# Q of five batches transposed by the DMA engines instead of by TensorE, with a new hand-written order, in a linear-attention and gated-FFN kernel

## Chip, cores and metric

The kernel runs on one core of one Trainium2 chip. The metric is the device time of one execution in microseconds. A profiled execution also has a span, from its first to its last instruction, which leaves out what lies around it.

## What is computed

There are 8 batches, 8 heads, 576 positions and a head dimension of 64. Cut to what matters:

```python
kv   = einsum('bhsd,bhse->bhde', k, v)          # per head 64 x 64
out  = einsum('bhsd,bhde->bhse', q, kv)
out  = out / sqrt(mean(out*out, -1) + 1e-6) * g_norm
x    = out.transpose(0, 2, 1, 3).reshape(B, S, 512)
h    = maximum(x @ w_in, 0)                     # 512 -> 1024
conv = sum over k of conv_w[k] * h[s + k - 1]   # 3 taps along the positions
y    = (h * sigmoid(conv)) @ w_out              # 1024 -> 512, float32
```

## The kernel before

All matmuls are in bfloat16 with float32 sums in PSUM. Features lie on the 128 partitions and positions along the free axis, so that two heads (a "pair" t of 0 to 3) fill the partitions. The work on a batch b is cut into small operations, each a function with a short name. A string ORDER (L64 to L109) lists them in the order in which they are recorded (the loop at L656), and a dependency from each instruction to the one before it on its engine (L661 to L669) keeps every engine's queue in just that order. The order comes from a planner; no engine passes one instruction by to run a later one. So a wait in any instruction holds all that stands behind it on its engine.

The operations, by the names in ORDER:

- `Lq.b`, `Lk.b.u`, `Lv.b.u` (L149 to L155) load q, k and v of a batch from DRAM. GpSimd's queue (POOL) issues them, and they cast float32 to bfloat16 on the way: one load reads 1,152 KB and writes 576 KB to 96 partitions, with six neighbouring positions in each partition's row. There are two buffers each for q, k and v, so the load of batch b waits until batch b-2 has been read.
- `qt.b.u` (L328 to L337) transposes q of four heads on TensorE, 24 matmuls against an identity into a PSUM tile of the pool `ps_a`. `qc.b.u` (L340) is VectorE's copy of it to SBUF, into a buffer named qT (four of them).
- `kv.b.t0.n` (L283) makes k-transposed times v, 12 matmuls for each pair, in PSUM. `kvc.b.t0.n.i` (L297) is ScalarE's copy of the two 64 x 64 diagonal blocks of each pair into a block-diagonal 128 x 128 matrix `kvbd`.
- `ot.b.t` (L351) makes the product of a pair: one 128 x 128 weight, 576 columns in two matmuls of 64 and 512 columns (`mm576`, L346).
- `sq`, `oc` (L383, L394) square and copy the product, on ScalarE; in the copy the positions are put in their natural order.
- Batch 0 is normalized with products by a matrix of ones (`on`, `nl`, `nx`, `mu0`), which need no sums over batches. For the others `ss` sums squares over a head on TensorE, `ln`, `ex` make the factor on ScalarE, and it is spread over the partitions in one of two ways: for batches 1 to 3 by TensorE (`sl`, `sp`, `mu`); for 4 to 7 through DRAM, `rw.g` (L501) writing it and `rr.b.t` (L506) reading it back broadcast with two DMAs from SP's queue, and `mr.b.t` (L516) multiplying.
- `hm.b.f` (L543) is the first FFN product, eight matmuls of 288 columns, and `re` (L546) its relu on ScalarE. `ta`, `ad`, `sg`, `mg` are the convolution, the sigmoid and the gate on VectorE and ScalarE (part of batch 0 by diagonal matrices on TensorE, `cv`, `sv`, `mv`). `om.p.m` (L626) is the last product, eight matmuls of 512 columns for 128 rows of a pair of batches p; `ea` copies it out on ScalarE and `st` (L645) stores it from SP's queue.
- `wu.n` (L651) are n idle matmuls[...].

`ps_a` has three buffers of two banks and `ps_b` two of one bank (L143, L144).

The code of before already holds the operations that the change turns on; with `XB = ()` none of them is recorded. They are shown with the change. The functions that use XB follow.

Of the kernel before, what the change touches and what calls it, by code (L numbers as in the profile page):

```python
# [63 lines left out]
ORDER = """  # L64
wu.6 cx Lq.1 cm cz di.1 di.2 Lk.1.0 Lv.1.0 Lk.1.1 Lv.1.1 cs wu.12 qt.0.0 qc.0.0 di.3 qt.0.1 kv.0.0.1
kvc.0.0.1.0 kvc.0.0.1.1 wu.2 ot.0.0 qc.0.1 oc.0.0 kv.0.1.1 sq.0.0 on.0.0 nl.0.0 kv.0.2.1 kvc.0.1.1.1
kvc.0.1.1.0 kvc.0.2.1.0 kvc.0.2.1.1 nx.0.0 ot.0.1 oc.0.1 sd.0.1 ot.0.2 sq.0.2 wu.3 on.0.2 kv.0.3.1 on.0.1
kvc.0.3.1.0 kvc.0.3.1.1 nl.0.2 nl.0.1 ot.0.3 sq.0.3 wu.4 on.0.3 nx.0.1 nx.0.2 ws.0 ws.1 nl.0.3 nx.0.3 mu0.0.0
mu0.0.1 mu0.0.2 wu.8 hs.0.0 mu0.0.3 hs.0.1 hm.0.0 hm.0.1 re.0.1 hm.0.3 re.0.0 re.0.3 ws.2 hm.0.4 hm.0.5 di.0
re.0.4 re.0.5 qt.1.0 qc.1.0 kv.1.0.2 hm.0.6 kvc.1.0.2.1 kvc.1.0.2.0 re.0.6 ot.1.0 qt.1.1 ot.1.1 kv.1.2.2 Lw  # L70
oc.1.0 sq.1.0 oc.1.1 kvc.1.2.2.1 ta.0.4 ta.0.5 qc.1.1 kvc.1.2.2.0 hm.0.7 sq.1.1 ot.1.2 ot.1.3 re.0.7 sq.1.2
sq.1.3 oc.1.3 hm.0.2 ss.1 ad.0.2 cv.0.0 re.0.2 ta.0.6 ta.0.7 cv.0.2 ad.0.3 ln.1 ex.1 sl.1 oc.1.2 sv.0.2 Lq.2
Lk.2.2 cv.0.1 Lv.2.2 Lq.3 sv.0.1 sv.0.0 wu.4 sp.1.1 mu.1.1 sp.1.0 Lk.3.2 Lv.3.2 sp.1.2 sg.0.2 sp.1.3 sg.0.3
mu.1.0 mu.1.2 mu.1.3 cv.0.3 qt.2.0 qc.2.0 mg.0.2 mv.0.0 hm.1.0 sv.0.3 hm.1.1 qt.2.1 kv.2.0.4 re.1.0 re.1.1
kvc.2.0.4.1 kvc.2.0.4.0 mg.0.3 mv.0.2 hm.1.7 qc.2.1 ot.2.2 re.1.7 oc.2.2 mv.0.1 Lq.4 Lk.4.2 ta.1.0 sq.2.2
ta.1.1 ad.1.0 hm.1.2 ot.2.3 hm.1.3 re.1.2 mv.0.3 qt.3.0 sq.2.3 oc.2.3 hm.1.5 ta.1.2 qc.3.0 re.1.3 ot.2.1
sg.1.0 re.1.5 hm.1.6 hm.1.4 oc.2.1 re.1.6 ot.2.0 ta.1.3 kv.3.0.4 ad.1.1 sq.2.1 sg.1.1 kvc.3.0.4.1 oc.2.0
kvc.3.0.4.0 sq.2.0 re.1.4 qt.3.1 mg.1.0 qc.3.1 ta.1.6 om.0.0 ea.0.0 ot.3.0 ot.3.3 mg.1.1 ot.3.1 ss.2 sq.3.3
sq.3.0 oc.3.0 oc.3.3 sq.3.1 om.0.1 ot.3.2 sq.3.2 oc.3.2 ea.0.1 qt.4.0 ss.3 qt.4.1 ta.1.4 ta.1.7 ln.2 ta.1.5
ad.1.3 ex.2 om.0.2 oc.3.1 ea.0.2 qc.4.0 ad.1.2 qc.4.1 Lv.4.2 Lq.5 Lk.5.2 Lv.5.2 Lq.6 kv.4.0.4 qt.5.1 qt.5.0  # L80
sl.2 qc.5.1 qc.5.0 kvc.4.0.4.0 sp.2.0 kvc.4.0.4.1 sp.3.0 mu.2.0 sp.2.2 mu.3.0 sp.3.3 sg.1.2 sg.1.3 mu.3.3
ot.4.3 mu.2.2 sp.2.1 sq.4.3 oc.4.3 Lk.6.2 Lv.6.2 ot.4.0 oc.4.0 ot.4.2 mu.2.1 mg.1.2 mg.1.3 ot.4.1 sq.4.0
oc.4.1 sq.4.1 kv.5.0.4 kvc.5.0.4.0 kvc.5.0.4.1 oc.4.2 sp.2.3 om.0.8 sq.4.2 mu.2.3 ot.5.2 sp.3.2 sq.5.2 oc.5.2
hm.2.0 st.0.2 st.0.0 mu.3.2 re.2.0 ea.0.8 sp.3.1 ss.4 ot.5.3 hm.2.1 sq.5.3 oc.5.3 re.2.1 mu.3.1 hm.3.0 re.3.0
# [8 lines left out]
re.4.2 hm.5.3 re.5.3 qc.7.0 hm.5.0 ot.7.2 re.5.0 sq.7.2 oc.7.2 mg.2.2 hm.5.1 hm.5.7 re.5.1 mg.2.3 re.5.7
ot.7.3 ot.7.0 om.1.7 ta.3.6 sq.7.0 sq.7.3 ta.3.0 ta.3.7 ot.6.3 oc.7.3 oc.7.0 ot.7.1 om.1.1 hm.5.2 ea.1.7
oc.6.3 sq.7.1 ta.3.1 st.0.5 sq.6.3 ea.1.1 oc.7.1 ad.3.3 st.1.1 ad.3.0 ss.6 re.5.2 ss.7 sg.3.3 hm.4.3 hm.5.5
hm.5.4 mg.3.3 ln.4 ex.4 re.4.3 om.1.2 om.1.6 rw.4 ta.3.2 ta.3.3 ea.1.2 re.5.4 sg.3.0 st.0.3 st.1.7 ad.3.1
hm.4.4 st.1.2 hm.4.5 ea.1.6 mg.3.0 rr.6.0 re.4.4 ta.3.4 mr.6.0 om.1.5 re.4.5 rr.6.3 rr.6.1 rr.6.2 ea.1.5
re.5.5 om.1.0 ea.1.0 ta.3.5 mr.6.3 st.1.5 om.1.3 sg.3.1 ea.1.3 mr.6.1 st.1.6 om.1.8 om.1.4 rr.7.1 mr.6.2
hm.6.0 ad.3.2 hm.6.4 mg.3.1 rr.7.3 mr.7.3 rr.7.0 mr.7.0 st.1.3 re.6.0 ea.1.8 hm.6.1 re.6.4 hm.6.7 re.6.1
ta.4.0 mr.7.1 hm.6.3 hm.6.6 sg.3.2 rr.7.2 re.6.3 mg.3.2 mr.7.2 ta.4.4 st.1.8 hm.6.2 re.6.7 hm.6.5 ta.4.1  # L100
re.6.6 re.6.2 re.6.5 hm.7.1 ta.4.5 re.7.1 hm.7.2 ea.1.4 hm.7.4 ad.4.0 re.7.2 st.1.4 re.7.4 ad.4.2 hm.7.5
hm.7.0 sg.4.0 hm.7.3 mg.4.0 re.7.5 ta.4.2 sg.4.2 mg.4.2 ta.4.3 hm.7.6 re.7.0 om.2.4 ad.4.1 ea.2.4 st.2.4
sg.4.1 ta.4.6 ta.4.7 hm.7.7 mg.4.1 ad.4.3 om.2.8 re.7.6 re.7.7 ea.2.8 ta.5.4 ta.5.5 om.2.2 ea.2.2 sg.4.3
om.2.0 ea.2.0 mg.4.3 st.2.8 ad.5.2 om.2.6 ea.2.6 st.1.0 sg.5.2 st.2.0 st.2.2 ta.5.0 om.2.3 ta.5.1 mg.5.2
ea.2.3 ad.5.0 om.2.7 ea.2.7 sg.5.0 om.3.3 ea.3.3 st.2.3 st.2.6 om.2.1 om.2.5 ea.2.1 re.7.3 st.3.3 ta.5.6
ta.5.7 mg.5.0 ad.5.3 sg.5.3 ea.2.5 st.2.7 ta.5.2 st.2.5 ta.5.3 ad.5.1 om.3.1 ea.3.1 sg.5.1 mg.5.3 st.2.1
# [593 lines left out]
```

## Time and profile before

| | |
|---|---|
| median of 3 runs | 194.04 us (193.19 to 194.55) |
| the profiled execution | 194.04 us |
| its span | 191.9 us |
| TensorE, matmuls | 177.9 us busy, 93% |
| VectorE | 156.1 us busy, 81% |
| ScalarE | 150.7 us busy, 79% |
| DMA queue that POOL issues | 17.30 MB written |
| DMA queue that SP issues | 14.47 MB written |

Reading it: the busy times are those of one execution, in which 2.1 us lie outside the span. A row of 40 digits gives the busy share of each fortieth of the span (4.8 us) in tenths. GB/s counts bytes written; the loads of q, k and v read twice as many. A matmul's duration in a row is its latency: in a stream they overlap, and a busy time divided by a count gives the pace. Engine names in the views are PE for TensorE, DVE for VectorE, ACT for ScalarE, POOL for GpSimd and SP for SyncE; a q behind one is its sequencer.

### The profile page before, as it was taken

What the parts mean: (1) busy time and instruction counts of PE and PEld (TensorE: products, weight loads), DVE (VectorE), ACT (ScalarE), POOL (GpSimd) and SP (SyncE); (2) the same over time, 40 slices, a digit from 0 to 9 for tenths busy, and PEclk for the clock granted to TensorE, in tenths of its full rate; (3) what the DMA queues carried; (4) which work ended last, traced back from release to release, by engine and by line L of the source; (5) the groups of instructions that cost most, each with busy time, mean ns of one, the idle gap of its engine ahead of it and who ended that gap; (6) DMA issues with size and microseconds to landing.
All of it is one profiled execution on the core that took longest, in us unless ns stands there. A gap on an engine that the chain in (4) does not pass through costs nothing.

```text
span 191.9 us, 4385 instructions
## 1 busy us (share of the span) xinstructions
PE 177.9 (93%) x1764; PEld 108.0 (56%) x1784; DVE 156.1 (81%) x314; ACT 150.7 (79%) x237; POOL 28.5 (15%) x41
## 2 busy tenths in 40 slices
PE   7969998899999779999999989999999999999992
...
DMA  4999999999999999994577300108865102424254
GB/s 54 200 282 324 203 204 206 204 204 206 201 205 202 205 249 204 220 234 84 149 214 238 115 0 3 56 19 277 263 205 144 55 3 94 183 109 169 107 220 164
DMA packets 30684, 32.05 MB, mean 167 GB/s; under 512 B 1712, under 2 KB 25544, under 8 KB 30664
## 3 DMA queue, kind: packets, MB, share of 16 engines
q0 software_dynamic: 20544, 17.30, 54.4%
q1 hardware_dynamic: 10120, 14.47, 22.8%
...
## 4 chain that ended last, share of the span: by engine, by line
PE 38%; ACT 19%; DVE 17%; DMA 13%; POOL 6%; issue 4%; SPq 2%; POOLq 0%; DVEq 0%; ACTq 0%
PE om_ps L631 21%; PE h_ps L534 12%; DMA v_sb<-in_v_dram 7%; DVE tap L566 5%; ACT h L547 4%; DMA rb<-scr 4%; ACT tap L580 4%; ACT o L400 3%; ACT L220 3%; DVE qT L342 3%; SPq L512 2%; ACT sq L385 2%; DVE tap L574 2%; DVE xT L517 2%; DVE xT L495 2%
## 5 line engine op out<-in xcount | busy, mean ns | idle before, releaser
L534 PE MATMUL h_ps<-xT,w_in_sb 128*128 128x288 bf16 x512 | 67.5, 286 | 2.0 <-ACT h L547 0.7
L631 PE MATMUL om_ps<-w_out_sb,h 128*128 128x512 bf16 x278 | 63.3, 379 | 0.6
L534 PEld LDWEIGHTS <-w_in_sb 128*128 128x128 bf16 x512 | 49.2, 98 | 17.5 <-issue 3.5
L566 DVE TENSOR_SCALAR tap<-h,cw 128x576 bf16<-128x576 bf16 (+1 forms) x132 | 47.4, 425 | 3.2 <-ACT h L547 2.8
L547 ACT ACTIVATE h<-h_ps 128x576 bf16<-128x576 f32 x64 | 40.2, 655 | 9.4 <-PE h_ps L534 9.1
L631 PEld LDWEIGHTS <-h 128*128 128x128 bf16 x288 | 27.9, 98 | 32.4 <-issue 0.6
L580 ACT ACTIVATE tap<-tap 128x1152 bf16<-128x1152 bf16 (+1 forms) x22 | 33.2, 1520 | 3.5 <-DVE tap L574 3.3
L637 ACT ACTIVATE row<-om_ps 128x512 f32<-128x512 f32 x36 | 21.6, 601 | 12.8 <-PE om_ps L631 9.8
L385 ACT ACTIVATE sq<-o_ps 128x576 bf16<-128x576 f32 x31 | 19.6, 657 | 4.2 <-DVE o L398 3.3
L574 DVE TENSOR_TENSOR tap<-tap 128x1150 bf16<-128x1150 bf16 (+1 forms) x22 | 21.6, 982 | 0.8
L586 DVE TENSOR_TENSOR h<-h,tap 128x1152 bf16<-128x1152 bf16 (+1 forms) x22 | 21.2, 969 | 0.9 <-ACT tap L580 0.9
L573 DVE TENSOR_TENSOR tap<-tap 128x1150 bf16<-128x1150 bf16 (+1 forms) x22 | 21.3, 969 | 0.0
L400 ACT ACTIVATE o<-o_ps 128x576 f32<-128x576 f32 x28 | 18.3, 666 | 0.2
L342 DVE COPY qT<-qt_ps 128x1152 bf16<-128x1152 bf16 x16 | 11.9, 752 | 6.7 <-PE qt_ps L335 6.7
L654 PE MATMUL wu_ps<-zeros 128*128 128x512 bf16 x38 | 12.7, 482 | 1.2 <-DVE zeros L173 1.2
L517 DVE TENSOR_TENSOR xT<-o,rb 128x576 bf16<-128x576 f32 x16 | 11.7, 753 | 1.2 <-DMA rb<-scr 1.0
L495 DVE TENSOR_TENSOR xT<-o,sp_ps 128x576 bf16<-128x576 f32 x12 | 8.5, 751 | 4.2 <-PE sp_ps L489 4.2
L153 POOL DMA_DIRECT2D q_sb<-in_q_dram x8 | 6.3, 793 | 32.9 <-PE qt_ps L335 29.9
L153 POOL DMA_DIRECT2D k_sb<-in_k_dram x12 | 9.4, 783 | 11.5 <-PE kv_ps L290 8.1
L335 PE MATMUL qt_ps<-ident,q_sb 96*64 96x96 bf16 x384 | 10.6, 207 | 0.3
L335 PEld LDWEIGHTS <-q_sb 96*64 96x64 bf16 x384 | 9.0, 110 | 2.6 <-issue 2.6
L153 POOL DMA_DIRECT2D v_sb<-in_v_dram x12 | 9.5, 795 | 0.4 <-DMA q_sb<-in_q_dram 0.4
...
## 6 DMA issues: line engine op xcount, KB each, us to landing
...
q_sb<-in_q_dram POOLq DMA_DIRECT2D x8, 576.0 KB, 12.3
...
k_sb<-in_k_dram POOLq DMA_DIRECT2D x6, 576.0 KB, 13.2
v_sb<-in_v_dram POOLq DMA_DIRECT2D x6, 576.0 KB, 15.4
...
```

The source lines that it names most:

```text
L153: nc.gpsimd.dma_start(out=qkv[name, b][:, h0:h0 + n, :], in_=src[b, h0:h0 + n].rearrange("h (p r) d -> p h (r d)", r=R))
L385: nc.scalar.activation(to, fr, AX.Square)
L400: nc.scalar.activation(to, fr, AX.Copy)
L534: nc.tensor.matmul(ps[:, e, :HS], w_in_sb[:, t, f * P:(f + 1) * P], x[:, t, e * HS:(e + 1) * HS], start=(t == 0), stop=(t == NT - 1))
L547: nc.scalar.activation(h_tile(b // 2)[:, f, b % 2, :].rearrange("p (e n) -> p e n", e=2), T["hm", b, f][:, :, :HS], AX.Relu)
L566: nc.vector.tensor_scalar_mul(tap[:, m, f % 2, :, :].rearrange("p b s -> p (b s)"), h_tile(p)[:, f, bs, :].rearrange("p b s -> p (b s)"), ...
L573: nc.vector.tensor_add(tap[:, 1, :, 1:], tap[:, 1, :, 1:], tap[:, 0, :, :S - 1])
L574: nc.vector.tensor_add(tap[:, 1, :, :S - 1], tap[:, 1, :, :S - 1], tap[:, 2, :, 1:])
L580: nc.scalar.activation(tap, tap, AX.Sigmoid)
L586: nc.vector.tensor_mul(h, h, T["tap", c, j][:, 1])
L631: nc.tensor.matmul(ps, h[:, f, m * P:(m + 1) * P], w_out_sb[:, f, :], start=(f == 0), stop=(f == NF - 1))
L637: nc.scalar.activation(T["os", p, m], T["om", p, m], AX.Copy)
```

## The change

XB becomes the batches 3 to 7, and ORDER is a new list. For a batch in XB:

- `xt.b.u` takes the place of `qt.b.u` and `qc.b.u`: one DMA that transposes q of four heads from SBUF (96 partitions x 1,536 elements, 294,912 bytes) to a qT buffer, issued from SP's queue. There are ten. In the result the partition holds the parity of the position (z) and the dimension, so a row holds 288 positions of one head.
- `kvs.b` and `kvx.b.i` take the place of the two `kvc.b`: three ScalarE copies (one of 128 partitions x 256 elements, two of 64 x 256) that lay out k-transposed times v of both heads in both halves of the partitions.
- `ot.b.t` becomes four matmuls of 64 x 64 weights and 288 columns, one for each head of the pair and each parity.
- `oc` and `sq` read the product with one more dimension in the access pattern.

```python
    @op
    def kvs(b):
        T["kvq", b] = kvq[b % 2]
        nc.scalar.activation(kvq[b % 2][:, :, 0, :], T["kvps", b, 0], AX.Copy)

    @op
    def kvx(b, i):
        fr, to = slice(i * D, (i + 1) * D), slice((1 - i) * D, (2 - i) * D)
        nc.scalar.activation(kvq[b % 2][to, :, 1, :], T["kvps", b, 0][fr], AX.Copy)


    @op
    def xt(b, u):
        T["qx", b, u] = work.tile([P, 4, HS], BF16, name="qT", bufs=BUFS["qT"])
        nc.sync.dma_start_transpose(
            out=T["qx", b, u].rearrange("p h (g n) -> p (h g) n", n=PS),
            in_=qkv["q", b][:, 4 * u:4 * u + 4, :].rearrange("p h n -> p (h n)"))
```

In `ot`, for a batch in XB:

```python
        for i in range(2):
            for z in range(2):
                rows = slice(z * D, (z + 1) * D)
                nc.tensor.matmul(
                    ps[i * D:(i + 1) * D, z * 512:z * 512 + HS], T["kvq", b][rows, t, z ^ i, :],
                    T["qx", b, t // 2][rows, 2 * (t % 2) + i, :], start=True, stop=True)
```

Totals by engine, counted in the built programs: TensorE has 144 transposes instead of 384, 80 of the 64 x 288 matmuls and 12 products of the old form instead of 32, and 36 idle matmuls instead of 39. VectorE has six `qc` copies instead of 16. ScalarE has two `kvbd` copies of 64 x 256 instead of 12, ten `kvx` and five `kvs`. SP issues ten DMAs more. POOL's queue is the same list of loads in the same order; but the loads of q for batches 5, 6 and 7 now wait for the transposing DMAs of batches 3, 4 and 5 instead of for TensorE. In SP's queue the transposes stand ahead of, or between, the first stores: xt of batches 3, 4 and 5, three stores, xt.6.1, a store, xt.7.0, xt.7.1, xt.6.0, and then `rw.3` and the `rr` reads.

The diff, cut to the first lines, the stretch from batch 2 to `hm.4.0`, and the last lines:

```diff
-ONES, KEEP, XB = ({0: (0, 1, 2, 3)}, ((0, 2), (0, 3)), ())
+ONES, KEEP, XB = ({0: (0, 1, 2, 3)}, ((0, 2), (0, 3)), (3, 4, 5, 6, 7))
 ORDER = """
-wu.6 cx Lq.1 cm cz di.1 di.2 Lk.1.0 Lv.1.0 Lk.1.1 Lv.1.1 cs wu.12 qt.0.0 qc.0.0 di.3 qt.0.1 kv.0.0.1
-kvc.0.0.1.0 kvc.0.0.1.1 wu.2 ot.0.0 qc.0.1 oc.0.0 kv.0.1.1 sq.0.0 on.0.0 nl.0.0 kv.0.2.1 kvc.0.1.1.1
...
-Lk.2.2 cv.0.1 Lv.2.2 Lq.3 sv.0.1 sv.0.0 wu.4 sp.1.1 mu.1.1 sp.1.0 Lk.3.2 Lv.3.2 sp.1.2 sg.0.2 sp.1.3 sg.0.3
-mu.1.0 mu.1.2 mu.1.3 cv.0.3 qt.2.0 qc.2.0 mg.0.2 mv.0.0 hm.1.0 sv.0.3 hm.1.1 qt.2.1 kv.2.0.4 re.1.0 re.1.1
-kvc.2.0.4.1 kvc.2.0.4.0 mg.0.3 mv.0.2 hm.1.7 qc.2.1 ot.2.2 re.1.7 oc.2.2 mv.0.1 Lq.4 Lk.4.2 ta.1.0 sq.2.2
-ta.1.1 ad.1.0 hm.1.2 ot.2.3 hm.1.3 re.1.2 mv.0.3 qt.3.0 sq.2.3 oc.2.3 hm.1.5 ta.1.2 qc.3.0 re.1.3 ot.2.1
-sg.1.0 re.1.5 hm.1.6 hm.1.4 oc.2.1 re.1.6 ot.2.0 ta.1.3 kv.3.0.4 ad.1.1 sq.2.1 sg.1.1 kvc.3.0.4.1 oc.2.0
-kvc.3.0.4.0 sq.2.0 re.1.4 qt.3.1 mg.1.0 qc.3.1 ta.1.6 om.0.0 ea.0.0 ot.3.0 ot.3.3 mg.1.1 ot.3.1 ss.2 sq.3.3
-sq.3.0 oc.3.0 oc.3.3 sq.3.1 om.0.1 ot.3.2 sq.3.2 oc.3.2 ea.0.1 qt.4.0 ss.3 qt.4.1 ta.1.4 ta.1.7 ln.2 ta.1.5
-ad.1.3 ex.2 om.0.2 oc.3.1 ea.0.2 qc.4.0 ad.1.2 qc.4.1 Lv.4.2 Lq.5 Lk.5.2 Lv.5.2 Lq.6 kv.4.0.4 qt.5.1 qt.5.0
-sl.2 qc.5.1 qc.5.0 kvc.4.0.4.0 sp.2.0 kvc.4.0.4.1 sp.3.0 mu.2.0 sp.2.2 mu.3.0 sp.3.3 sg.1.2 sg.1.3 mu.3.3
-ot.4.3 mu.2.2 sp.2.1 sq.4.3 oc.4.3 Lk.6.2 Lv.6.2 ot.4.0 oc.4.0 ot.4.2 mu.2.1 mg.1.2 mg.1.3 ot.4.1 sq.4.0
-oc.4.1 sq.4.1 kv.5.0.4 kvc.5.0.4.0 kvc.5.0.4.1 oc.4.2 sp.2.3 om.0.8 sq.4.2 mu.2.3 ot.5.2 sp.3.2 sq.5.2 oc.5.2
-hm.2.0 st.0.2 st.0.0 mu.3.2 re.2.0 ea.0.8 sp.3.1 ss.4 ot.5.3 hm.2.1 sq.5.3 oc.5.3 re.2.1 mu.3.1 hm.3.0 re.3.0
-ot.5.1 sq.5.1 oc.5.1 hm.3.1 hm.3.2 re.3.1 re.3.2 ot.5.0 sq.5.0 hm.2.2 re.2.2 oc.5.0 hm.3.5 ta.2.0 ta.2.1
-ad.2.0 re.3.5 ss.5 hm.3.3 ln.3 ta.2.2 hm.2.3 re.2.3 qt.6.0 qc.6.0 kv.6.0.4 re.3.3 ta.2.3 qt.6.1 hm.2.4 hm.3.4
-ex.3 sg.2.0 kvc.6.0.4.1 qc.6.1 hm.2.5 re.2.4 re.2.5 re.3.4 ad.2.1 om.0.4 st.0.8 st.0.1 rw.3 hm.2.7 kvc.6.0.4.0
-ea.0.4 rr.4.0 hm.3.7 mg.2.0 re.2.7 hm.2.6 hm.3.6 re.3.7 sg.2.1 Lq.7 Lk.7.2 Lv.7.2 re.3.6 re.2.6 ta.2.4 mr.4.0
-ta.2.5 rr.5.3 rr.4.3 mr.5.3 mr.4.3 rr.4.1 ot.6.1 mr.4.1 rr.5.1 rr.4.2 rr.5.0 mg.2.1 ad.2.2 om.0.7 mr.4.2
-ot.6.2 ea.0.7 ot.6.0 sq.6.0 om.0.3 st.0.4 sq.6.1 om.0.6 ea.0.3 oc.6.0 oc.6.1 sq.6.2 oc.6.2 ta.2.6 ea.0.6
-sg.2.2 om.0.5 kv.7.0.4 mr.5.1 mr.5.0 ea.0.5 rr.5.2 hm.4.0 ta.2.7 st.0.6 re.4.0 kvc.7.0.4.0 hm.4.1 hm.4.6
...
-om.3.2 ea.3.2 om.3.0 ea.3.0 st.3.0 st.3.1 mg.5.1 om.3.6 st.3.2 ea.3.6 st.3.6 om.3.5 ea.3.5 om.3.4 ea.3.4
-st.3.4 om.3.8 ea.3.8 st.3.8 st.3.5 om.3.7 ea.3.7 st.3.7
+wu.6 cx cz di.2 cs di.3 di.0 wu.12 qt.0.0 di.1 qt.0.1 qc.0.0 Lq.1 Lk.1.0 kv.0.0.1 kvc.0.0.1.1 Lv.1.0 Lk.1.1
+Lv.1.1 Lw Lq.2 kvc.0.0.1.0 wu.2 ot.0.0 sq.0.0 qc.0.1 kv.0.1.1 kvc.0.1.1.1 kvc.0.1.1.0 wu.2 ot.0.1 oc.0.0
...
+Lk.3.2 ta.0.4 Lv.3.2 sq.1.3 hm.0.3 sq.1.2 ta.0.5 ad.0.2 ss.1 re.0.3 cv.0.3 ln.1 ex.1 ta.0.6 ta.0.7 ad.0.3
+oc.1.2 oc.1.3 sl.1 wu.1 cv.0.1 sv.0.3 sv.0.1 qt.2.0 qc.2.0 sp.1.1 mu.1.1 sp.1.3 mu.1.3 cv.0.0 sp.1.0 sp.1.2
+sv.0.0 sg.0.3 sg.0.2 mu.1.0 mu.1.2 qt.2.1 cv.0.2 sv.0.2 mg.0.2 qc.2.1 mv.0.0 hm.1.4 re.1.4 kv.2.0.4
+kvc.2.0.4.0 xt.3.0 hm.1.5 kvc.2.0.4.1 ot.2.3 re.1.5 ot.2.1 mg.0.3 mv.0.3 sq.2.1 oc.2.1 sq.2.3 ta.1.4 ta.1.5
+ad.1.2 hm.1.0 oc.2.3 re.1.0 hm.1.1 ot.2.2 hm.1.7 oc.2.2 re.1.1 re.1.7 ot.2.0 oc.2.0 mv.0.2 mv.0.1 sq.2.2
+hm.1.6 kv.3.0.4 re.1.6 sq.2.0 kvx.3.1 kvx.3.0 kvs.3 om.0.0 sg.1.2 Lq.4 Lk.4.2 ot.3.0 xt.3.1 ot.3.2 ot.3.1
+ea.0.0 sq.3.0 oc.3.0 om.0.3 Lv.4.2 Lq.5 Lk.5.2 ta.1.0 ot.3.3 sq.3.1 om.0.1 xt.4.0 xt.4.1 mg.1.2 ea.0.3 sq.3.2
+Lv.5.2 sq.3.3 oc.3.1 ea.0.1 ta.1.1 ss.2 ss.3 ln.2 ex.2 hm.1.2 re.1.2 om.0.2 hm.1.3 ad.1.0 ta.1.6 ta.1.7 ad.1.3
+ea.0.2 oc.3.3 sl.2 sp.2.0 oc.3.2 re.1.3 sp.3.3 sg.1.0 sp.2.2 kv.4.0.4 mu.2.0 mu.3.3 sp.3.0 mu.2.2 mu.3.0
+sp.2.1 sp.2.3 sp.3.2 xt.5.0 mu.2.3 xt.5.1 kvx.4.1 mu.2.1 kvx.4.0 kvs.4 st.0.3 sp.3.1 sg.1.3 mu.3.1 mu.3.2
+mg.1.3 st.0.1 ot.4.0 ot.4.1 st.0.0 oc.4.0 sq.4.0 oc.4.1 sq.4.1 kv.5.0.4 ta.1.2 hm.2.0 hm.2.5 ta.1.3 ad.1.1
+mg.1.0 kvs.5 kvx.5.0 kvx.5.1 re.2.0 hm.3.0 re.2.5 re.3.0 ot.5.2 hm.3.4 sg.1.1 hm.2.4 re.3.4 oc.5.2 sq.5.2
+re.2.4 hm.2.1 ta.2.4 ot.4.3 re.2.1 ot.4.2 hm.3.5 sq.4.3 oc.4.3 hm.3.1 sq.4.2 re.3.5 mg.1.1 oc.4.2 ss.4 ot.5.3
+re.3.1 ot.5.0 ot.5.1 sq.5.3 ta.2.5 om.0.5 sq.5.0 sq.5.1 oc.5.1 oc.5.3 ss.5 hm.3.7 hm.2.6 ad.2.2 oc.5.0 ea.0.5
+hm.3.6 sg.2.2 ta.2.0 ta.2.1 om.0.4 ln.3 mg.2.2 ex.3 re.3.7 re.2.6 ad.2.0 re.3.6 om.0.7 hm.2.7 hm.3.2 ea.0.7
+ea.0.4 re.2.7 hm.2.2 sg.2.0 hm.2.3 re.2.3 re.2.2 ta.2.6 Lq.6 Lk.6.2 Lv.6.2 Lq.7 Lk.7.2 xt.6.1 kv.6.0.4 ta.2.7
+ad.2.3 st.0.2 xt.7.0 kvx.6.0 xt.7.1 om.0.6 kvx.6.1 xt.6.0 rw.3 rr.4.0 mr.4.0 rr.4.2 rr.4.3 Lv.7.2 mg.2.0
+rr.4.1 st.0.7 kvs.6 hm.3.3 ot.6.3 mr.4.3 mr.4.2 kv.7.0.4 rr.5.1 re.3.2 ta.2.2 ea.0.6 mr.4.1 re.3.3 ot.6.0
+ot.6.1 om.0.8 sq.6.3 oc.6.3 st.0.4 oc.6.1 sq.6.1 sg.2.3 hm.4.0 hm.4.5 ta.2.3 mr.5.1 ad.2.1 re.4.0 sq.6.0
...
+sg.5.2 mg.5.3 st.2.3 om.3.2 ea.3.2 om.3.0 ea.3.0 st.2.8 st.3.2 mg.5.2 st.2.4 om.3.7 ea.3.7 st.3.0 om.3.5
+ea.3.5 st.3.5 om.3.6 ea.3.6 om.3.4 ea.3.4 st.3.7 st.3.4 st.3.6 om.3.8 ea.3.8 st.3.8
```

41 lines of the change are left out of this document (20 added, 21 removed).

## The prediction

> **What bounds the kernel now.** I read the page first: busy times, forty slices, chain.
>
> ```profile
> span 191.9 us, 4385 instructions
> ...
> PE   7969998899999779999999989999999999999992
> ...
> DMA  4999999999999999994577300108865102424254
> GB/s 54 200 282 324 203 204 206 204 204 206 201 205 202 205 249 204 220 234 84 149 214 238 115 0 3 56 19 277 263 205 144 55 3 94 183 109 169 107 220 164
> ```
>
> Two resources are full. TensorE is, from about 70 us to the end; and until 86 us (18 slices of 4.8 us) so are the DMA engines, at a flat 204 GB/s written: the loads of q, k and v. Do the loads set the pace there? The DMA view of a short window gives issue to landing of one load (last column); the timeline gives the issue and the kv product that needs the load (start, duration, ...). Batch 5:
>
> ```profile
> v_sb<-in_v_dram POOLq DMA_DIRECT2D x1, 576.0 KB, 14.2
> ```
>
> ```profile
> 56.00 0.79 POOL L153 DMA_DIRECT2D v_sb<-in_v_dram  x1
> ...
> 71.44 1.07 PE L290 MATMUL kv_ps<-v_sb,k_sb 96*64 96x64 bf16 x48
> ```
>
> v of batch 5 lands at 56.00 + 14.2 = 70.2 us, and kv.5 starts at 71.44. By the same views v of batches 2 and 3 lands at 43.0 and 51.8, and kv starts at 43.56 and 52.7. Batch 4 has 2.7 us to spare, batch 6 has 7, batch 7 has 15. So up to kv.5 the kernel walks behind the load stream; after it the loads are ahead. What follows kv.5 is the view of busy times by stretch (PE, PEld, DVE, ACT, POOL, clock, DMA share, GB/s):
>
> ```profile
> 71.44:188.30 116.86, 114.95 (x940) 70.13 (x950) 99.12 (x168) 94.72 (x139) 1.53 (x2) 1.00 0.51 140
> ```
>
> TensorE works 114.95 of the 116.86 us from kv.5 to the last matmul. So the end is the start of kv.5 plus TensorE's work behind it.
>
> **What the skill says.** (1) The Trainium skill, "DMA: Bandwidth & Descriptors", section "Issuing engines are not separate DMA queues": all DMAs run on the same 16 engines and interleave. The trace agrees. k of batch 5 lands at 55.24 + 11.0 = 66.2, so v came 4.0 us behind it, and q of batch 6 (61.63 + 11.8 = 73.4) 3.2 us behind v; loads alone follow each other by 2.9 (0.59 MB at 204 GB/s). In between ran two stores of 256 KB: 1.4 us lost, 0.7 each. (2) Same page, section "Latency and other measured facts": a transposing DMA moved 261 GB/s with a non-contiguous middle dimension, 350 to 400 if contiguous. No transposing DMA is in this trace. (3) "TensorE: Matmul & The Clock Gate", section "Part 3: Packing small matmuls — row/col tiling": matmuls in different row and column groups run at once. The trace shows it for columns: eight 288-column matmuls of `ss` span 0.43 us, where eight of `h_ps` span 1.14. (4) "TensorEngine Tiling (Array Packing)", "Key Properties": a change of tiling mode drains the array; the trace shows no separate row for it.
>
> **The change, part by part.** Let x be the time by which one transposing DMA sets the load stream back.
>
> ```profile
> L342 DVE COPY qT<-qt_ps 128x1152 bf16<-128x1152 bf16 x16 | 11.9, 752 | 6.7 <-PE qt_ps L335 6.7
> ...
> L335 PE MATMUL qt_ps<-ident,q_sb 96*64 96x96 bf16 x384 | 10.6, 207 | 0.3
> ```
>
> *Transposes and order, behind kv.5.* 10.6 us for 384 is 27.6 ns each, and the chain has 0.65 us for 24: take 0.62 a tile. Ten tiles leave, 6.2 us, but six stand before kv.5, where TensorE waits for loads anyway. Behind kv.5 four leave (batches 6 and 7): -2.5. The order moves work across kv.5: one `om` (8 x 0.219, from 49 matmuls in 10.74 us in the chain, = 1.75) and three `sp` pairs (0.25 each) go ahead of it, two `ot` (0.25) behind it: -2.0. Sum -4.5 us.
>
> *Product.* Now two matmuls, 0.03 + 0.22 = 0.25 us in the chain. Four 64 x 64 tiles of 288 columns take 0.13 if all run together (a 288-column matmul streams in 0.13), 0.53 if none do. I take 0.25: together, plus a drain on both sides. Fourteen of the twenty stand behind kv.5: between -1.7 and +3.9, taken 0.
>
> *VectorE.* Ten copies of 0.75 leave, 7.5 us; four behind kv.5. It is busy 99.12 of 116.86 there, so they buy nothing directly. Its last gate ends at 179.3 with five `om` (8.8 us) behind it, so it has no room to be late; but it can run ahead while TensorE waits for v.
>
> *ScalarE.* Three copies for two, 0.375 us each in their row: +0.4 a batch, +1.9 in all. Hidden under TensorE (94.72 of 116.86 busy); uncovered it would cost those 1.9. The permuted reads of `oc` and `sq` stay at 0.66: an estimate, same elements.
>
> *Idle matmuls, start.* 36 for 39, in gaps: kv.1 waits for v of batch 1 until 26.4 either way, as POOL's loads are the same list in the same order. Zero.
>
> *DMA traffic.* 294,912 bytes at the stores' 0.7 us for 262,144 is 0.8; at the page's 261 GB/s, 1.13. I take x = 1.13. Lower bound 0 (if the transposes fit beside loads that are bound by DRAM; the stores speak against it), upper 2 (small pieces, a guess at twice the price). By v of batch 5, q of batches 3, 4 and 5 has landed, so six transposes are in the stream. Against that, the wait after landing shrinks from 1.2 to 0.2 (kv.1 started 0.04 after its load), and SP's queue now puts three stores, not two, behind xt.5.1 and ahead of v: +0.5. kv.5 moves by 6x - 1.0 + 0.5 = +6.3 us, to 77.7. The idle TensorE also loses clock for a few us; it did at 68 to 72 too (0.6 there), so nothing more.
>
> *SP's queue.* `rw.3` now stands behind xt.7.0, xt.7.1 and xt.6.0. xt.7.0 waits for q of batch 7, which landed at 65.85 + 17.8 = 83.7; plus eight transposes 92.7. Three issues of 0.6 (median of `rb`; its longest is 1.7) put `rw.3` at 94.5 to 97.8. Its data, `ex.3`, ended at 87.5; with kv.5's 6.3 and 1.3 less work in between, 92.5. So it starts 2 to 5 us late. Behind it: 2.3 for the write, eight `rr` issues at 0.74 (14 in 10.40), 3.6 to landing, 0.75 for `mr.4.1`: 12.5, and then hm.4.0. From `ex.3` to hm.4.0 the new order holds 13.4 us of matmuls, 14.3 of ScalarE. Late by 0.2 to 4; taken 1.2. What is queued behind: hm.4.0 and all of TensorE. The loads of q wait for transposes now, but 8 us of loads are in the stream at any time, so POOL's wait costs nothing.
>
> Sum: +6.3 - 4.5 + 0 + 1.2 = +3.0 on the span of 191.9: 194.9. With 2.1 us around it, 197.0. The profiled execution's 194.04 is also the median.
>
> **Rivals.**
> *Paced by loads (forecast)*: for it, the landings a microsecond ahead of kv.2, kv.3 and kv.5. Against it, the new order puts kv.5 as early in TensorE's work as before. x of 0.8 to 1.5: 194 to 200.
> *Not slower: the transposes hardly slow the loads.* x decides: 6x - 0.5 = 4.5 at x = 0.83 without the SP wait. At x = 0 kv.5 keeps its place and 4.5 us of matmuls are gone, 1.7 more if the product packs: 194.04 - 4.5 - 1.7 = 187.8 to 189.5. At x = 0.5 (kv.5 +2.5) 192.0. For it: they read no DRAM.
> *SP's queue is the bound*: `rw.3` 4 us late, issues of 1.7 us: 197 + 2.8 = 199.8. For it: three DMAs and two waits ahead of it; against: DVE waited only 1.0 us for `rb` before.
> *Slow transposes or a serial product*: x = 2 adds 5.2 (202.2); serial matmuls add 3.9 (200.9).
> *The change doesn't do what it says*: excluded; the transposes are gone from the built program.
>
> **How the numbers follow.** Forecast 0.45; transposes nearly free 0.2; between the two (x near 0.7, 192 to 196) 0.15; SP's queue 0.1; slow or serial 0.1. Likeliest 197.0, its own range 194 to 200. Over all cases 190 to 204, which leaves a tenth on each side. About 1% is what a measurement can tell from no change (192.1 to 196.0): faster 0.2; same 0.2 (all of the middle, a little of the forecast); slower 0.6.
>
> **What would show it.** Right: TensorE idle before kv.5 with v of batch 5 as releaser, kv.5 at 76 to 79; about 112 us from kv.5 to the last matmul; landings of v more than 10 us per batch apart from batch 3 on, against 8.6. Product: `o_ps` groups of four in about 0.25. SP: `rw.3` after `ex.3` by 2 us or more, VectorE waiting for `rb`. Wrong: kv.5 before 74 us, or landings still 8.6 apart (x is small), or TensorE's idle time elsewhere.

## The result, and the profile after

The changed kernel takes 215.59 us (median of 4 runs, 214.32 to 216.50) where the kernel before takes 194.30 (4 runs beside them). The ratio is 1.110, with a 95% interval of 1.102 to 1.118: slower by 21.3 us. The forecast of 197.0 had the sign and was 18.6 us short; its range ended at 204. The profiled execution has a span of 212.0 us against 191.9.

The page of the changed kernel, the lines that answer to those of before:

```profile
span 212.0 us, 4004 instructions
...
PE   7887687798507997989995189999999999999992
...
PEclk9999999999965999999999659999999999999999
DMA  4999999999999999999993781002588102533533
GB/s 63 200 312 275 200 207 204 205 203 190 189 163 133 190 195 156 241 167 218 199 144 122 228 288 35 0 2 100 207 259 225 36 0 99 194 111 145 199 148 148
DMA packets 42522, 34.97 MB, mean 165 GB/s; under 512 B 13552, under 2 KB 37384, under 8 KB 42504
```

A slice is now 5.3 us. TensorE has two holes that were not there before: slices 11 and 12 (digits 5 and 0, 53 to 64 us) and slices 22 and 23 (5 and 1, 111 to 122 us). The granted clock falls to 0.5 to 0.6 in or just after each. The flat 204 GB/s of the loads is gone from the tenth slice on: 190, 189, 163, 133. There are 11,838 more packets than before, all under 512 bytes by the same line of its page (1,712 there), 1,184 for each of ten transposes of 294,912 bytes.

The view of busy times by stretch (PE, PEld, DVE, ACT, POOL, clock, DMA share, GB/s), cut at kv.4, kv.5 and the two holes:

```profile
54.23:57.01 2.78, 2.73 (x55) 1.61 (x56) 0.00 (x0) 1.77 (x4) 0.00 (x0) 1.00 1.27 190
57.01:65.00 7.99, 0.38 (x9) 0.21 (x12) 6.13 (x14) 2.10 (x4) 0.00 (x0) 0.67 1.32 148
65.00:77.66 12.66, 12.25 (x73) 5.16 (x74) 2.49 (x6) 8.82 (x15) 3.08 (x4) 0.80 1.25 183
...
112.00:123.00 11.00, 3.32 (x35) 1.53 (x29) 5.68 (x9) 4.42 (x6) 0.00 (x0) 0.76 0.63 195
123.00:142.00 19.00, 17.90 (x117) 11.29 (x117) 15.94 (x23) 16.48 (x26) 0.00 (x0) 0.87 0.22 68
142.00:208.05 66.05, 65.12 (x383) 36.15 (x387) 55.90 (x105) 47.04 (x67) 0.00 (x0) 1.00 0.41 139
```

The holes are 7.6 and 7.7 us of idle TensorE. From 142 us to the end it is full, as before. What ended the waits stands in TensorE's timeline (start, duration, ..., idle before and releaser):

```profile
54.23 0.95 PE L289 MATMUL kv_ps<-v_sb,k_sb 96*64 96x64 bf16 x48 [1.53 <-DMA v_sb<-in_v_dram]
...
58.92 0.32 PE L359 MATMUL o_ps<-qT,kvq 64*64 64x288 bf16 x4 [1.91 <-DMA qT<-q_sb]
64.94 0.69 PE L359 MATMUL o_ps<-qT,kvq 64*64 64x288 bf16 x8 [5.70 <-DMA qT<-q_sb]
65.57 3.60 PE L630 MATMUL om_ps<-w_out_sb,h 128*128 128x512 bf16 x8
...
77.66 0.95 PE L289 MATMUL kv_ps<-v_sb,k_sb 96*64 96x64 bf16 x48
...
82.05 0.95 PE L289 MATMUL kv_ps<-v_sb,k_sb 96*64 96x64 bf16 x48
```

The first hole is ot.3: TensorE waits not for a load but for the transposed q of batch 3. The `om` right behind it takes 3.60 us where one takes 1.89; the granted clock is 0.50 from 65.0 to 69.2. kv.4 is at 77.66, though v of batch 4 landed at 66.0. kv.5 is at 82.05, 10.6 us later than before, and nothing is named as its releaser: it did not wait for v. The second hole begins in SP's queue, whose timeline is:

```profile
46.90 32.61 SPq L322 DMA_TRANSPOSE qT<-q_sb  x6
...
100.75 7.57 SPq L322 DMA_TRANSPOSE qT<-q_sb  x3
108.41 0.87 SPq L502 DMA_DIRECT2D scr<-rs  x1
112.44 5.25 SPq L511 DMA_DIRECT2D rb<-scr  x8
```

`ex.3` was done at 102.0. `rw.3` (L502) stands behind three transposes and goes out at 108.41, its write lands 4.0 us later, and VectorE and then TensorE wait for what is read back:

```profile
116.27 0.76 DVE L516 TENSOR_TENSOR xT<-o,rb 128x576 bf16<-128x576 f32 x1 [7.03 <-DMA rb<-scr]
```

```profile
122.79 2.56 PE L533 MATMUL h_ps<-xT,w_in_sb 128*128 128x288 bf16 x10 [4.38 <-DVE xT L516]
```

The view of the tile qT in SP's queue has the price of a transpose, issue first (ns, min/median/max), then from issue to landing:

```profile
L322 SPq DMA_TRANSPOSE qT<-q_sb x10: 1350/3194/5917, 46.9 to 107.0; - x10
...
DMA to landing us min/median/max: 5.1/9.4/15.7
```

The product is as it was taken. A row of its four matmuls is 0.32 us, which is latency; the next work starts 0.25 us after it where nothing is waited for (86.32 to 86.57, 111.03 to 111.28), as behind the two matmuls of before.

### The profile page after: what moved, and what is told of

It is laid out like the page before. It is cut to its first block, busy times and chain, and to the rows that moved or that the text cites. A ratio compares the mean times of both kernels' runs of the same rounds, so it can differ in the third digit from the quotient of the medians.

```text
span 212.0 us, 4004 instructions
## 1 busy us (share of the span) xinstructions
PE 176.1 (83%) x1563; PEld 102.3 (48%) x1581; DVE 149.7 (71%) x304; ACT 153.3 (72%) x242; POOL 27.9 (13%) x41
## 4 chain that ended last, share of the span: by engine, by line
PE 41%; ACT 27%; DMA 18%; POOL 5%; issue 3%; DVE 2%; SPq 2%; POOLq 0%; ACTq 0%; DVEq 0%
PE om_ps L630 24%; PE h_ps L533 14%; DMA qT<-q_sb 7%; ACT h L546 7%; DMA v_sb<-in_v_dram 7%; ACT tap L579 5%; ACT o L399 4%; ACT sq L384 3%; ACT L219 2%; DMA scr<-rs 2%; ACT row L636 2%; SPq L511 2%; DMA rb<-scr 2%; POOL k_sb L152 1%; POOL v_sb L152 1%
## 5 line engine op out<-in xcount | busy, mean ns | idle before, releaser
L533 PE MATMUL h_ps<-xT,w_in_sb 128*128 128x288 bf16 x512 | 71.5, 293 | 11.8 <-DVE xT L516 4.4
L630 PE MATMUL om_ps<-w_out_sb,h 128*128 128x512 bf16 x275 | 65.4, 387 | 1.4 <-issue 0.5
L533 PEld LDWEIGHTS <-w_in_sb 128*128 128x128 bf16 x512 | 50.3, 100 | 31.8 <-issue 15.7
L546 ACT ACTIVATE h<-h_ps 128x576 bf16<-128x576 f32 x64 | 40.2, 660 | 13.9 <-PE h_ps L533 13.3
L384 ACT ACTIVATE sq<-o_ps 128x576 bf16<-128x576 f32 x31 | 20.1, 684 | 8.0 <-PE o_ps L359 6.6
L572 DVE TENSOR_TENSOR tap<-tap 128x1150 bf16<-128x1150 bf16 (+1 forms) x22 | 21.3, 969 | 0.0
L516 DVE TENSOR_TENSOR xT<-o,rb 128x576 bf16<-128x576 f32 x16 | 11.7, 753 | 8.5 <-DMA rb<-scr 8.5
L359 PE MATMUL o_ps<-qT,kvq 64*64 64x288 bf16 x80 | 6.4, 324 | 9.2 <-DMA qT<-q_sb 7.9
L152 POOL DMA_DIRECT2D k_sb<-in_k_dram x12 | 8.9, 740 | 20.2 <-PE kv_ps L289 16.1
L653 PE MATMUL wu_ps<-zeros 128*128 128x512 bf16 x34 | 10.3, 441 | 1.2 <-DVE zeros L172 1.2
L289 PE MATMUL kv_ps<-v_sb,k_sb 96*64 96x64 bf16 x384 | 8.3, 197 | 2.3 <-DMA v_sb<-in_v_dram 2.3
L289 PEld LDWEIGHTS <-k_sb 96*64 96x64 bf16 x384 | 7.3, 112 | 4.8 <-issue 4.6
L359 PEld LDWEIGHTS <-kvq 64*64 64x64 bf16 x80 | 2.5, 107 | 14.0 <-issue 6.5
```

Of the source, the lines that this page charges most:

```text
L152: nc.gpsimd.dma_start(out=qkv[name, b][:, h0:h0 + n, :], in_=src[b, h0:h0 + n].rearrange("h (p r) d -> p h (r d)", r=R))
L384: nc.scalar.activation(to, fr, AX.Square)
L533: nc.tensor.matmul(ps[:, e, :HS], w_in_sb[:, t, f * P:(f + 1) * P], x[:, t, e * HS:(e + 1) * HS], start=(t == 0), stop=(t == NT - 1))
L546: nc.scalar.activation(h_tile(b // 2)[:, f, b % 2, :].rearrange("p (e n) -> p e n", e=2), T["hm", b, f][:, :, :HS], AX.Relu)
L572: nc.vector.tensor_add(tap[:, 1, :, 1:], tap[:, 1, :, 1:], tap[:, 0, :, :S - 1])
L630: nc.tensor.matmul(ps, h[:, f, m * P:(m + 1) * P], w_out_sb[:, f, :], start=(f == 0), stop=(f == NF - 1))
```

## Experiments

The theory after the result: a transposing DMA is slow, and costs in three places, at ot.3 (TensorE waits for it), in POOL's queue (the loads of q wait for it and the stream runs dry) and in SP's queue (rw.3 stands behind it). Rivals: the new order by itself costs the time; the new product does; the POOL wait is hidden. All ratios are to the kernel before on the same chip, with 95% intervals.

**The new order alone.**

```diff
-ONES, KEEP, XB = ({0: (0, 1, 2, 3)}, ((0, 2), (0, 3)), (3, 4, 5, 6, 7))
+ONES, KEEP, XB = ({0: (0, 1, 2, 3)}, ((0, 2), (0, 3)), ())
-... xt.b.u ... kvs.b kvx.b.0 kvx.b.1
+... qt.b.u qc.b.u ... kvc.b.0.4.0 kvc.b.0.4.1
```

> The new order with no transposing DMA: q of batches 3 to 7 is transposed by TensorE again (24 matmuls and a VectorE copy per half batch, XB empty), each where a PSUM buffer is free at about the old distance ahead of its ot. Theory (the transposing DMAs cost the time, not the order): about 193, between 190 and 197. Rival (the new order itself costs it, for example the three stores ahead of kv.5 or the om before it): 208 or more.

206.72 us, ratio 1.063 (1.058 to 1.068). Neither theory, and nearer to the rival: the order without one transposing DMA loses 12 us. But I had put the transposes of batch 6 where VectorE waited for them ahead of the rb products (4.85 us in this trace; the 6.5 of the next expectation is its wait at 59 us, for an earlier batch), so I mended that:

```diff
-... ta.2.6 Lq.6 Lk.6.2 Lv.6.2 qt.6.1 qc.6.1 qt.6.0 qc.6.0 Lq.7 ... kv.6.0.4
+kv.5.0.4 Lq.6 Lk.6.2 Lv.6.2 Lq.7 ... oc.5.1 qt.6.0 qc.6.0 ... oc.5.0 qt.6.1 qc.6.1 ... kv.6.0.4
```

> The run with the new order alone, with one thing mended: in it TensorE's transposes and VectorE's copies of batch 6 stood right before kv.6, where VectorE waited 6.5 us for them ahead of the rb products. Here they stand behind oc.5.1 and oc.5.0, 10 us earlier; the loads of batch 6 and of q of batch 7 stand earlier in POOL's queue, which holds nothing else. If the order itself costs the 12.9 us of that run: 204 to 207. If the place that was given to the transposes of batch 6 cost part of it: 198 to 203.

203.70 us, ratio 1.047 (1.040 to 1.054). This leaves at most 4.7% to the order, with its transposes placed by hand and not by a planner.

**The transposing DMAs in the order of before.**

```diff
-... qt.b.u qc.b.u ... kvc.b.0.4.i      (order of before, b = 3 to 7)
+... xt.b.u ... kvs.b kvx.b.i
```

> The order of the kernel before, with each PE transpose of batches 3 to 7 replaced on the spot by a transposing DMA, and the four-tile product. Theory: the transposes are slow wherever they stand, so 205 or more, with TensorE waiting for qT in each batch, as they now stand close to their ot. Rival (order): about 194 to 198.

209.40 us, ratio 1.078 (1.073 to 1.083). The transposes, with the product that goes with them, cost 15 us without any new order. The product rival is tested next, in the order of before, with TensorE transposing 128 columns at once for batches 2 to 7 and no xt:

```diff
+        if b in XB:
+            for h in range(4):
+                for g in range(3):
+                    at = (h % 2) * HS + g * PS
+                    nc.tensor.transpose(ps[:, h // 2, at:at + PS],
+                                        q_sb[:, 4 * u + h, g * P:(g + 1) * P], ident[:PS, :PS])
```

> The kernel before in its own order, no transposing DMA, but the product of the change: for batches 2 to 7 TensorE transposes 128 columns of q (two token parities of a head) at once, 12 matmuls a half batch for 24, and the product is the four 64 x 64 tiles. If the product costs what the profile of the changed kernel shows (0.25 to 0.32 for four) and the transposes half of 0.62: about 192 to 194. If the permuted reads or the third copy on ScalarE cost more than the profile shows: 195 or more.

196.22 us, ratio 1.009 (1.006 to 1.012). The upper case, by a little, so this version does not beat the kernel before. The wide transposes bring nothing (144 in 7.8 us, 54 ns each, for 27.6 ns each before), so the 1.7 us are the price of the product and its copies on six batches: a small part of a loss of 21 us at most.

**rw.3 ahead of the transposes of batch 7.**

```diff
-... st.0.2 xt.7.0 ... xt.7.1 ... xt.6.0 rw.3 rr.4.0 ... rr.5.2
+... st.0.2 xt.6.0 ... rw.3 rr.4.0 ... rr.5.2 xt.7.0 xt.7.1
```

> The changed kernel with three tokens moved: xt.6.0 one step earlier (behind st.0.2), xt.7.0 and xt.7.1 behind rr.5.2, so that rw.3 and the rb reads of batches 4 and 5 stand ahead of the wait for q of batch 7 in SP's queue. Theory (rw.3 stands behind slow transposes and the wait for q7, about 7 us): 207 to 210. If that wait only hides another one (TensorE late anyway): 213 to 216.

210.37 us, ratio 1.083 (1.076 to 1.090): 2.7% of 194.3, 5.2 us, come back. Not the whole hole: rw.3 now goes out at 103.79, right after `ex.3`, but its write lands 5.4 us later (2.35 before). xt.6.0 still stands ahead of it, issued at 92.3 and landed at 107.2, and loads run beside it.

**Three buffers for q.** The first try made room with three row buffers for four.

```diff
-'q': 2, ... 'row': 4
+'q': 3, ... 'row': 3
```

> The changed kernel with three buffers for q instead of two, and three row buffers for the output instead of four, to make room. POOL's load of q of batch 5 then needs not wait for the transposes of batch 3. Theory (the dry load stream of 4 to 5 us sets kv.5 late): v of batch 5 lands 4 us or more earlier, kv.5 at 78 or before instead of 82, and 210 to 213 in all. Rival (POOL's wait costs nothing, the transposes take the same DMA time sooner or later): kv.5 stays at 81 to 83, 215 to 216.

219.69 us, ratio 1.133 (1.128 to 1.138). Slower, and for another reason. ScalarE's timeline:

```profile
84.25 0.60 ACT L636 ACTIVATE row<-om_ps 128x512 f32<-128x512 f32 x1 [10.08 <-DMA out_dram<-row]
```

An `ea` waited 10.1 us for a row buffer whose store stood behind a transpose in SP's queue. The next one keeps four rows:

```diff
-'q': 2, ... 'row': 4 ... 'rs': 2
+'q': 3, ... 'row': 4 ... 'rs': 1
-    zeros = consts.tile([P, NT, P], BF16, name="zeros")
+    zeros = consts.tile([P, 1, P], BF16, name="zeros")
```

> The changed kernel with three buffers for q, and this time four row buffers as before; the room comes from one rs buffer for two and a 128-wide tile of zeros for the idle matmuls instead of a 512-wide one. In the run with three rows ScalarE waited 10.1 us for a row whose store stood behind a transpose in SP's queue, so it says nothing on q. Theory (POOL's wait of 18.5 us lets the load stream run dry and makes v of batch 5 late): v of batch 5 lands by 75 instead of 78.8, kv.5 at 76 to 79, 209 to 213 in all. Rival (loads and transposes share the same DMA time, so loads that start earlier make the transposes as much later): kv.5 at 81 to 83, 214 to 217.

214.31 us, ratio 1.101 (1.093 to 1.110), which is that of the changed kernel (1.102 to 1.118). The theory falls here. v of batch 5 in the changed kernel (POOL's timeline, and the DMA view of that issue, last column to landing):

```profile
65.47 0.77 POOL L152 DMA_DIRECT2D q_sb<-in_q_dram  x1 [18.50 <-DMA qT<-q_sb]
...
67.06 0.78 POOL L152 DMA_DIRECT2D v_sb<-in_v_dram  x1
```

```profile
v_sb<-in_v_dram POOLq DMA_DIRECT2D x1, 576.0 KB, 11.7
```

and the same two views with three q buffers:

```profile
55.67 0.78 POOL L152 DMA_DIRECT2D v_sb<-in_v_dram  x1 [0.38 <-issue]
```

```profile
v_sb<-in_v_dram POOLq DMA_DIRECT2D x1, 576.0 KB, 23.2
```

Issued 11.4 us earlier, v lands at 55.67 + 23.2 = 78.9 instead of 67.06 + 11.7 = 78.8. The transposes and the loads share the DMA engines, and one in front makes the other late. POOL's wait of 18.5 us cost nothing.

**The price of a transpose by itself.** The kernel before, with transposes that nobody reads:

```diff
+    def xd(i):
+        nc.sync.dma_start_transpose(
+            out=xs[i].rearrange("p h (g n) -> p (h g) n", n=PS),
+            in_=w_in_sb[:PS].rearrange("p t f -> p (t f)")[:, :4 * R * D])
-... ws.2 ... st.0.7 ... st.1.1
+... ws.2 xd.0 xd.1 ... st.0.7 xd.0 xd.1 ... st.1.1 xh.0
```

> The kernel before, untouched, plus five transposing DMAs in SP's queue whose result nobody reads: two of the full size (96 x 1536) from w_in_sb at about 30 us, beside loads; two more at about 107 us, where the DMA engines are idle; one of half the size at about 124 us. Theory (a transpose is slow by itself): 4.5 to 6 us to landing each and in series where nothing else runs, half of that for the half size; beside loads each sets the load stream back by 2.5 us or more, so v of batch 2 lands 5 us later and the kernel takes 196 to 200. Rival (cheap by itself, as the forecast had it: 1.1 us each): 2 to 3 us to landing alone, v of batch 2 later by 2.3, kernel 194 to 196.

200.08 us, ratio 1.028 (1.020 to 1.035), at the upper edge of what the theory gave. Beside the loads the two took 13.3 and 17.5 us to landing (issued at 23.2 and 25.6). The pair at 110 us (window of that stretch in the view of the tile xs):

```profile
DMA to landing us min/median/max: 4.4/4.6/4.8
```

TensorE's timeline of the same run:

```profile
48.42 0.95 PE L290 MATMUL kv_ps<-v_sb,k_sb 96*64 96x64 bf16 x48 [2.17 <-DMA v_sb<-in_v_dram]
...
76.78 0.95 PE L290 MATMUL kv_ps<-v_sb,k_sb 96*64 96x64 bf16 x48
```

kv.2 was at 43.56 before and is 4.86 us later, 2.43 for each transpose. That is a lower bound, as kv.2 did not wait before: v of batch 2 itself landed at 48.3 instead of 43.0, 2.65 for each. kv.5 is 5.3 us later, and the last matmul 4.7. So the two at 23 us carry the whole cost, and the three in the idle stretch cost nothing. The trace has no landing for the one of half the size, so whether half the size takes half the time stays open.

**Batch 3 back on TensorE**, without and with rw.3 first:

```diff
-(3, 4, 5, 6, 7)
+(4, 5, 6, 7)
-... xt.3.0 ... kvx.3.1 kvx.3.0 kvs.3 ... xt.3.1
+... qt.3.0 qc.3.0 ... kvc.3.0.4.0 kvc.3.0.4.1 ... qt.3.1 qc.3.1
```

> The changed kernel with batch 3 alone back on TensorE's transposes and the ordinary product (24 matmuls and a VectorE copy where xt.3.0 and xt.3.1 stood); batches 4 to 7 stay with the transposing DMA. Three q buffers moved no end, so POOL's wait and the dry load stream are out as the cause of the late kv.5; what is left is that TensorE itself stood 7.6 us at ot.3 for the transpose of q of batch 3. Theory: without that wait kv.5 at 75 to 78 instead of 82, and 209 to 212 in all. Rival (the load stream slowed by transposes sets kv.5, TensorE's stop at ot.3 only stands in front of it): kv.5 at 80 or later, 214 or more.

> The same, and xt.6.0, xt.7.0 and xt.7.1 moved as in the run with rw.3 first. Theory (two separate losses, TensorE at ot.3 and rw.3 behind the transposes, which add up): 203 to 206, near the 203.7 of the new order with no transposing DMA. Rival (they overlap): 207 or more.

207.53 us, ratio 1.066 (1.061 to 1.070), and 207.62 us, ratio 1.069 (1.066 to 1.072). Without the wait at ot.3 the end comes earlier by 4.4%, 8.6 us, more than expected. The second gain does not add up with it: with rw.3 first the time is the same. TensorE's timeline of the run with both:

```profile
75.47 1.32 PE L289 MATMUL kv_ps<-v_sb,k_sb 96*64 96x64 bf16 x48 [1.70 <-DMA v_sb<-in_v_dram]
...
87.25 0.45 PE L359 MATMUL o_ps<-qT,kvq 64*64 64x288 bf16 x4 [6.23 <-DMA qT<-q_sb]
```

kv.5 comes at 75.47 instead of 82.05, now behind v (5.7 us of the 6.6 if one counts from kv.1, which was 0.9 earlier in this execution); and the wait for a transpose has moved on to ot.5, 6.2 us. The wait at ot.3 was what set kv.5, and the transposes of the next batches stand ready to take its place.

**Only batches 6 and 7**, first in the order of before:

```diff
-... qt.6.u qc.6.u ... qt.7.u qc.7.u
+... st.0.1 xt.6.0 xt.6.1 rw.3 ... rr.5.2 xt.7.0 xt.7.1
```

> The order of the kernel before, transposing DMAs for batches 6 and 7 alone, which have 7 and 15 us to spare on their loads: xt.6.0 and xt.6.1 behind st.0.1 in SP's queue (about 78 us), xt.7.0 and xt.7.1 behind rr.5.2 (about 102 us), where transposes that nobody waited for cost nothing. Theory (a transpose costs only where loads pace the kernel, where TensorE waits for it, or where something urgent stands behind it in SP's queue): 191.5 to 194, as 2.5 us of TensorE leave from behind kv.5; rw.3 may be late by an issue. Rival (they cost wherever they stand): 197 or more.

> The same for batch 7 alone. Theory: 192.5 to 194, as 1.2 us of TensorE leave and SP's queue has nothing urgent behind rr.5.2. Rival: 195 or more.

198.57 us, ratio 1.021 (1.018 to 1.025), and 195.97 us, ratio 1.008 (1.004 to 1.012). Both fall where the rivals had them, 197 or more and 195 or more, so the theory that late transposes are free in this order falls. In the first, SP's timeline and TensorE's:

```profile
87.99 0.34 SPq L503 DMA_DIRECT2D scr<-rs  x1
94.89 1.34 SPq L512 DMA_DIRECT2D rb<-scr  x2
```

```profile
109.27 9.18 PE L534 MATMUL h_ps<-xT,w_in_sb 128*128 128x288 bf16 x60 [2.75 <-DVE xT L517]
```

rw.3 was issued 0.5 us later than before, but its write took 6.9 us instead of 2.35, behind two transposes in the same queue, the second of which landed at 94.6; TensorE paid 2.75. For batch 7 alone no wait of that kind is in the trace. TensorE's timeline has

```profile
105.88 0.95 PE L290 MATMUL kv_ps<-v_sb,k_sb 96*64 96x64 bf16 x48
...
115.73 0.32 PE L360 MATMUL o_ps<-qT,kvq 64*64 64x288 bf16 x4 [0.96 <-ACT h L547]
```

This kv.7 is 1.8 us later than before. 1.5 of that arose between kv.5 and kv.6, where the clock was 0.78 from 71.8 to 80 us (1.00 before): ahead of the first transpose, at 104.0, so not its doing. From kv.7 to the last matmul it takes 84.1 us for 84.2, where 1.2 less was expected; the wait of 0.96 us for a relu of ScalarE is new. Whether ScalarE's third copy makes it was not tested.

Then in the new order, with batches 3 to 5 by TensorE as in the order alone, and xt.6.0, xt.7.0, xt.7.1 placed as in the run with rw.3 first:

> The new order with transposing DMAs for batches 6 and 7 alone, xt.6.0 behind st.0.2 and xt.7.0 and xt.7.1 behind rr.5.2; batches 3 to 5 are transposed by TensorE, placed as in the run of the order alone. Theory (the early six, where TensorE waits for them, carry the cost of the transposes; the new order costs the rest): 202 to 205, at the 203.7 of the order without any transposing DMA or a little under. Rival (late transposes cost as much, as they delay the writes and reads of the row scales in SP's queue): 207 or more.

199.55 us, ratio 1.028 (1.021 to 1.035), better than either theory. It differs from the run with rw.3 first only in batches 3 to 5. The view by stretch of this run, to kv.2, to kv.5 and to the last matmul:

```profile
0.00:44.83 44.83, 36.20 (x409) 21.02 (x414) 29.12 (x90) 29.04 (x53) 19.94 (x30) 0.96 1.17 207
44.83:77.06 32.23, 27.80 (x426) 17.34 (x429) 24.39 (x50) 25.55 (x44) 6.80 (x9) 1.00 1.20 193
77.06:193.73 116.67, 112.54 (x849) 66.47 (x860) 100.29 (x172) 96.90 (x144) 1.63 (x3) 1.00 0.59 146
```

and of the kernel before, to kv.2 and to kv.5:

```profile
0.00:43.56 43.56, 38.09 (x422) 22.29 (x427) 30.42 (x93) 29.49 (x55) 19.33 (x29) 0.96 1.17 209
43.56:71.44 27.88, 24.84 (x414) 15.56 (x413) 26.58 (x55) 25.92 (x44) 7.69 (x10) 0.94 1.30 212
```

kv.5 comes 5.6 us later, and behind it the stretch is as long as before (116.67 against 116.86). 1.2 of the 5.6 were there at kv.1 already, which waits for v of batch 1 and came between 26.4 and 27.7 in the profiled executions of both orders; that is not the order's cost. The rest is. The new order has 1.9 us less of TensorE's work ahead of kv.2, which gains nothing (kv.2 is at 43.48 in the order alone, 43.56 before), and 3.0 us more between kv.2 and kv.5, where the kernel before idles only 3.04 us in all; 1.4 us more idle time comes on top.

The order alone, with all transposes on TensorE, also loses behind kv.5: from 76.50 to its last matmul are 121.50 us.

```profile
76.50:198.00 121.50, 115.16 (x929) 69.02 (x940) 102.71 (x176) 96.74 (x142) 1.64 (x3) 1.00 0.47 129
```

So in the new order the four late transposes by DMA did better than those that were placed by hand on TensorE (1.028 against 1.047; the loads of batch 6 stand elsewhere too), while in the order of before they lost 2.1%.

The loss, step by step along one path:

| step | ratio | worth, of 194.3 us |
|---|---|---|
| the changed kernel | 1.110 | |
| rw.3 ahead of the transposes of batch 7 | 1.083 | 5.2 us |
| and batches 3 to 5 by TensorE | 1.028 | 10.6 us |
| and the order of before, all by TensorE (the kernel before) | 1.000 | 5.5 us |

The last step is two changes, the order and the four late transposes. And the shares hold for this path only: with batch 3 on TensorE first, worth 8.6 us, rw.3 first was worth nothing. Each ratio is good to 0.7 points, so each share to about 2 us.

## Why the prediction was wrong

*What bounds the kernel.* It said that up to kv.5 the kernel walks behind the load stream. That was read from landings about 1 us ahead of kv.2, kv.3 and kv.5. TensorE's timeline of before does not bear it out:

```profile
26.41 0.57 PE L290 MATMUL kv_ps<-v_sb,k_sb 96*64 96x64 bf16 x24 [0.33 <-DMA v_sb<-in_v_dram]
...
43.56 0.92 PE L290 MATMUL kv_ps<-v_sb,k_sb 96*64 96x64 bf16 x48
```

kv.1 waits for its load. kv.2 and all that follow name no releaser: their loads came just in time, and TensorE was at work until then. Between kv.2 and kv.5 TensorE was busy 24.84 of 27.88 us, and VectorE 26.58. The step that failed first is the one built on this, that work of the new order ahead of kv.5 is free because TensorE waits for loads there. The order alone puts kv.5 at 76.50, 5.1 us late, without one transposing DMA.

*The size of x.* Taken as 1.13 us, with 2 as the upper bound. The added transposes measure 2.43 to 2.65 beside loads. The Trainium skill's "DMA: Bandwidth & Descriptors", section "Latency and other measured facts", has 261 GB/s for a transposing DMA; in the idle stretch this one moved 294,912 bytes in 4.6 us from issue to landing, 64 GB/s, and the measurement decides. 294,912 bytes in 1,184 packets are 249 bytes each. The same page's section "Issuing engines are not separate DMA queues", which the prediction leaned on, has all DMAs share the same 16 engines. The trace agrees: the load of v that went out 11.4 us earlier landed at the same time. v of batch 5 landed at 78.8, late by 8.6 where the sum gave 7.3 (6x + 0.5). That this came near is luck: x was too small, and only four of the six transposes had landed by then (those of batch 5 were issued at 72.6 and 74.6 and landed at 83.2 and 86.1).

*Who waits for a transpose.* This step was missing. The prediction priced a transpose only as a delay of the loads, never as a result that ot.3 needs. xt.3.1 was issued at 49.2 and landed at 64.9, and TensorE stood 7.6 us for the two of batch 3, with half a clock behind. With batch 3 on TensorE kv.5 comes 6.6 us earlier. So +6.3 for kv.5 was measured +10.6, and by another mechanism than v of batch 5, which landed 3 us ahead of kv.5. Of the signs to look for, the landings more than 10 us apart are there (54.2, 66.0, 78.8 for v of batches 3 to 5); v as releaser of kv.5, on which the sum rests, is absent.

*TensorE behind kv.5, -4.5.* The transposes of batches 6 and 7 are gone as forecast: 112.54 us busy in the last run against 115.16 in the order alone, -2.6 for -2.5. The -2.0 for moved work did not come (115.16 against 114.95 before). In the changed kernel TensorE is busy 114.67 us there; work at the lower clock behind the second hole is in that. kv.5 to the last matmul is 126.0 us, where 112 was forecast.

*Product 0.* Right on TensorE: 0.25 us for four, as taken. With its copies it cost 1.7 us on six batches in the order of before; what of that is TensorE's and what ScalarE's is open.

*SP's queue, +1.2.* The mechanism was right and the size was not. Late by 2 to 5 was said; rw.3 went out 6.4 us after `ex.3`, as an issue took 1.35 to 5.9 us and not 0.6 to 1.7. Not seen at all: the write that follows lands late as well, 4.0 us for 2.35, right behind the last transpose ahead of it (issued at 107.0, landed at 112.1). Putting it first gives 5.2 us back in the changed kernel.

*POOL's wait costs nothing.* Right in its verdict, though the wait was 18.5 us long and the load stream ran nearly dry (v of batch 4 landed at 66.0, the next load went out at 65.47), and not for the reason given: what is not loaded then is transposed then.

*Rivals.* "Slow transposes" stopped at 2 us and 202.2 and changed only x. With 2.43 the same sum gives 197.0 + 6 x 1.30 = 204.8, and with 2.65 it gives 206.1, still 9 to 11 short: the kinds of cost were missing, not only their size. "SP's queue is the bound" had the place of the second hole.

What stays open: why a single late pair of transposes in the order of before loses 0.8% in the median instead of gaining, how the new order loses behind kv.5 when TensorE transposes, and how much of the order's 5.5 us a planner would win back if it were given the measured prices. To issue the transposes from another queue than SP's was not tried.
